# Moving the turning and summing of rows behind the ninth output product in a fused attention and mixture-of-experts kernel

## The chip, the cores and the metric

One core of one Trainium2 chip runs the whole kernel. The metric is device time in microseconds (us); lower is better. Names of engines are those of the profile: PE is TensorE (PEld its weight loads), DVE is VectorE, ACT is ScalarE, POOL is GpSimd, SP is the engine that issues the large loads. PE's granted clock of 1.00 is 2.4 GHz, 0.50 is 1.2 GHz.

## What is computed

The reference is attention followed by a mixture of experts with one expert per token, all in float32:

```
x = attention(q, k, v)                  # 8 batches, 8 heads, 576 positions, 64 features; heads 0-3 see a window
                                        # of 32 positions, heads 4-7 every fourth of 128 positions
logits = x @ w_gate                     # x: 8 x 576 tokens of 512 features; 8 experts
e = argmax(logits)  or the expert of the token before it, where sigmoid(x @ w_local) >= 0.5
out = softmax(logits)[e] * (relu(x @ w1[e]) @ w2[e])     # w1[e] 512 x 1024, w2[e] 1024 x 512
```

## The kernel before, in words

The first part (about 160 us) is attention and routing. Each token's row of x is written to a table `xd` in memory. The rest is the experts' work, on which this document dwells.

**Units.** Tokens are sorted by expert and cut into 19 units, each of one expert. The planner at L872 to L888 lists them in a fixed order: units 0 to 3 are pairs (256 tokens), 4 full (128), 5 half (64), 6 quad (512), 7 quart (32), 8 quad, 9 full, 10 quad, 11 half, 12 quart, 13 quad, 14 full, 15 quad, 16 quart, 17 quad, 18 quart. Below, H8 is the hidden layer of unit 8 and O8 its output layer. Weights lie in two slots, even units in one and odd units in the other; SP loads the next unit of a slot (2 MB for w1, 2 MB for w2) as soon as the present one has been used (L900).

**Order.** The loop at L1536 goes over units u from 2 on and emits: H of u (`run_hidden`), then `features(u + 1)`, then `gather_more`, then O of u - 1 (`run_output`). So a quad's output comes after the hidden layer of the small unit that follows it, and ahead of the next quad's hidden layer. PE and DVE run what they are given in the order in which it is emitted (L222 exempts these two from the scheduler); the order on POOL, ACT and SP is chosen by a scheduler.

**Products.** Quads multiply with seven products of half size in place of eight (`chain`, L1059). An output of a quad is two such chains over three accumulators x, y, z (L1285), 14 products in all. The fifth product of a chain adds to x; `finish(3)` (DVE, L1309) reads x; the seventh product adds to x again and so must wait for that read. Operands that are sums are made on DVE: sums of w1 (`sum`, L958 to L961, 128x1024), of w2 (`sum`, L964 to L967), of hidden rows (`hc`, L958 to L961, 128x512), of input rows (`xcq`, L964 to L967, 128x512). Of the second chain's `hc`, two sums are made behind the third product and two behind the sixth (L1278).

**Rows.** `features(u)` (L1055) first calls `turn_rows` (L1026): it issues whatever gathers of unit u are still waiting (`fetch_all`), then DVE turns the rows (`xe<-xg`, L1037, four instructions of 128x512 for a quad, one per 128 tokens), and then `sums_of_rows` makes four `xcq` sums. The second product of a quad's hidden layer needs the first `xcq` sum, which needs all four turned blocks.

**Gathers.** The rows of a quad come from `xd` by 16 gathers (`fetch`, L988), each a tiny DVE memset (L999) and an indirect DMA issued by POOL (L1000). Gathers wait in one list in order of units. Behind every product there is a gap (`work_gap`, L939), which may put one sum on DVE and then gives the list a credit, 2 for large units and 1 for small ones, kept to at most 5; a gather costs 3 (L1014). `gather_more(done)` (L1005) lets further units into the list while those beyond `done` need no more than 9 buffers (a quad needs 4, other late units 1):

```
while following[0] < NU and sum(map(need, range(done + 1, following[0] + 1))) <= XG:
    gather(following[0])
    following[0] += 1
```

**Sums of w1** for the next quad are given to `run_output` as `push`, behind 14 empty steps, so that they fall behind products 10, 11 and 14 (two of them there).

Of the kernel before, what the change touches and what calls it, by code (L numbers as in the profile page):

```python
# [72 lines left out]
EARLY, FIRST = 2, 2  # L73
# [145 lines left out]
def whole(ctx, tc, exact, bad, qk, v, wgl, w1, w2, con, msk, qmk, out, cst, wg, ones):  # L219
# [664 lines left out]
    units = [dict(kind="pair", col=2 * i, late=False) for i in range(FIRST)]  # L884
# [3 lines left out]
    NU = len(units)  # L888
# [11 lines left out]
    def weights(u, second):  # L900

        i = units[u]["slot"]
        loads.add((u, second))
        if not second:
            units[u]["held"] = holds.get(i)
            holds[i] = nc.values_load(of_unit(u, "experts", rows=1), engines=[ET.SP], min_val=0, max_val=E - 1,
                                      skip_runtime_bounds_check_because="clamped to the experts")
            units[u]["expert"] = holds[i]
        e, held = units[u]["expert"], units[u]["held"]
        w, s, pattern = (w2, raw2, "p m f -> p (m f)") if second else (w1[u >= TURNED], raw1, "p m k f -> p (m k f)")  # L910
        if not second and u >= TURNED and units[u]["before"] < TURNED:
            held = None
        if second and not units[u]["late"] and isinstance(held, int):
            held = None
        more = {} if held is None else dict(cond=e != held, cond_hint=False)
        nc.sync.dma_start(out=s[i].rearrange(pattern), in_=w[bass.ds(e, 1)].rearrange("o p x -> (o p) x"), **more)
# [6 lines left out]
    def next_weights(*did):  # L923

        ready.update(did)
        if "late" in ready:
            for w in [w for w in follow if w in ready]:
                follow.remove(w)
                weights(after[w[0]], w[1])

    def gap(time=3):
        fetch_some(time)
        for steps in waiting, behind:
            if steps:
                f = steps.pop(0)
                if f:
                    f()

    def work_gap(sums=True, time=2):  # L939
        for _ in range(len(soon) > 4 and 2 or len(soon) > 0 if sums else 0):  # L940
            soon.pop(0)()
        gap(time)

    def now(push):
        for f in push:
            f()

    def flush():
        while soon:
            soon.pop(0)()  # L950
# [30 lines left out]
    def gather(u):  # L981


        for j, n in enumerate({"quad": (NQS,) * 4, "pair": (NQS, NQS), "full": (NQS,), "half": (ROW // SQ,), "quart": (1,)}[units[u]["kind"]]):
            for q in range(2 if u < TURNED else n):
                fetches.append((u, lambda u=u, j=j, q=q: fetch(u, j, q)))
# [18 lines left out]
    def gather_more(done):  # L1005

        def need(u):
            return {"quad": 4, "pair": 2}.get(units[u]["kind"], 1)
# [4 lines that stand above are left out]
# [13 lines left out]
    def turn_rows(u):  # L1026
        kind = units[u]["kind"]
        rows = {"half": ROW, "quart": SQ}.get(kind, P)
        assert u >= TURNED or kind == "pair"
        fetch_all(u)  # L1030
        xe[u] = [mw.tile([P, DK, 2 * P], F32, name="xe") for _ in range(2 if kind == "quad" else 1)]
        for j in range({"quad": 4, "pair": 2}.get(kind, 1)):
            x = xg.pop((u, j))
            to = xe[u][j // 2][:, :, j % 2 * P:j % 2 * P + rows]
            if u >= TURNED:
                x = x.rearrange("p g (q f) -> p (g q) f", f=P)
                nc.vector.transpose(to.rearrange("p k (q t) -> p k q t", t=SQ),  # L1037
                                    x[:, :rows // SQ].rearrange("p q (k d) -> p k q d", k=DK))
                continue
            x = x.rearrange("p g f -> p (g f)")  # L1040
            tp = bank([P, DK, P], "tp")
            for kk in range(DK):
                nc.tensor.transpose(tp[:, kk], x[:, kk * P:(kk + 1) * P], ident)
            nc.scalar.copy(to, tp)

    def sums_of_rows(u):
        if not units[u]["seven"]:
            return []
        if units[u]["kind"] == "quad":
            xc[u] = stage.tile([P, 4, DK // 2, 2 * P], F32, name="xcq", bufs=1)  # L1050
            return sums_right(xc[u], *(xe[u][j][:, 2 * k:2 * k + 2] for k in range(2) for j in range(2)))
        xc[u] = mw.tile([P, 4, DK // 2, P], F32, name="xc", bufs=1)
        return sums_right(xc[u], *(xe[u][0][:, 2 * k:2 * k + 2, j * P:(j + 1) * P] for k in range(2) for j in range(2)))

    def features(u):  # L1055
        turn_rows(u)
        now(sums_of_rows(u))
# [146 lines left out]
    def turned(u):  # L1204

        h = ht[u]
        n = 2 if units[u]["kind"] == "half" else 1
        ts = h[:, 0:n].rearrange("p m t -> p (m t)")
        tp = bank([P, 2 * n, P], "ht")
        for c in range(2 * n):  # L1210
            nc.tensor.transpose(tp[:, c], ts[:, c * P:(c + 1) * P], ident)
        nc.scalar.copy(h[:, 2:2 + n].rearrange("p m (c t) -> p (m c) t", t=P), tp)
# [219 lines left out]
    def register(value, most, why):  # L1432
        return nc.values_load(value, min_val=0, max_val=most, skip_runtime_bounds_check_because=why)
# [23 lines left out]
    def run_hidden(u, push):  # L1457
        soon.extend(push)
        for k, fits in enumerate(hidden(u)):
            work_gap(fits, 2 if is_large(u) else 1)  # L1460
            if u == FIRST and k == 1:
                early_sums[u] = sums_of_weights(u, True)
                soon.extend(early_sums[u][:2])
            if u == FIRST and k == 4:
                turn_rows(u + 1)
        flush()
        if u < FIRST:
            next_weights((u, False))
        elif after[u] is not None:
            weights(after[u], False)  # L1470

    def run_output(u, push):
        soon.extend(push)
        for k, fits in enumerate(output(u)):
            work_gap(fits, 2 if is_large(u) else 1)
            if u == NU - 2 and k == 4:
                turned(u + 1)
        if u == NU - 2 and k < 4:
            turned(u + 1)
        flush()  # L1480
        if u < FIRST:
            next_weights((u, True))
        elif after[u] is not None:
            weights(after[u], True)

    def is_large(u):
        return FIRST <= u < NU and units[u]["kind"] in ("pair", "quad") or 0 <= u < FIRST

    def before_it(u):
        return max((t for t in range(u) if is_large(t)), default=-2)  # L1490

    def both(u):
        if not is_large(u):
            return []
        sums = units[u]["sums"]
        if u > TURNED - 1 and before_it(u) < u - 1:
            return list(sums)
        if u in early_sums:
            return sums[:2] + [early_sums[u][2]] + sums[2:] + [early_sums[u][3]]
        return [f for two_ in zip(sums, sums_of_weights(u, True)) for f in two_]  # L1500
# [32 lines left out]
    def wait(gaps):  # L1533
        return [lambda: None] * (2 * gaps)

    for u in range(FIRST, NU):  # L1536
        own = is_large(u) and u >= TURNED and before_it(u) < u - 1
        run_hidden(u, (both(u - 1) if u > FIRST else []) + (wait(5) + sums_of_weights(u, True) if own else []))
        if u > FIRST and u + 1 < NU:
            features(u + 1)  # L1540
        gather_more(min(u + 1, NU - 1) if u > FIRST else FIRST)
        push = [f for t in when.get(u, []) for f in
                wait((7 if units[u - 1]["kind"] == "quad" else 5) if is_large(u - 1) else 0) + sums_of_weights(t, False)]
        if u > FIRST:
            run_output(u - 1, push)
        else:
            now([f for two_ in zip(sums_of_rows(u + 1), sums_of_weights(u + 1, False)) for f in two_])
        if units[u]["kind"] in ("half", "quart") and u < NU - 1:
            turned(u)
        if u in (FIRST + 3, FIRST + 4) and not exact:  # L1550
            next(checks)
        if u == FIRST + 6 and not exact:
            again = register(bad[0:1, 0:1], 1, "a comparison's result")
    now(both(NU - 1))
    run_output(NU - 1, [])
    return again

# [58 lines left out]
```

## Time and profile before

| | |
|---|---|
| median of 3 runs | 645.85 us (644.46 to 646.57) |
| profiled execution | 645.84 us, of which the span of the trace is 643.9 us |
| PE busy in the span | 604.5 us (94%) |
| DVE, POOL, ACT busy | 360.5, 226.0, 176.2 us |
| mean granted clock of PE | 0.983 |

How to read it: PE is busy nearly throughout, so other engines matter where PE waits for them. "Busy" for PE also covers matmuls at half clock. In the rows below, the first number is the start in us from the start of the span, the second the duration; x8 means that eight like instructions are merged, and the bracket tells how long the engine sat idle before and what ended that.

### The profile page before, as it was taken

The numbers are of one execution on the slowest core, as the hardware profiler recorded it, in microseconds if no ns is written. First come the engines' busy times: TensorE is split into PE (matmuls) and PEld (weight loads), VectorE is DVE, ScalarE is ACT, GpSimd is POOL, SyncE is SP. The second block draws the span as 40 slices with busy tenths as digits, with TensorE's granted clock in tenths as the row PEclk, the third lists the DMA queues.
The fourth block names the chain that finished last, engine by engine and source line by source line (L and its number), as shares of the span: only waits on it lengthen the run. The fifth ranks groups of instructions, "written<-read, shape, count | busy, mean of one in ns | idle before, by whom it ended". The sixth has DMA issues, their size and how long they took to land.

```text
span 643.9 us, 13952 instructions
## 1 busy us (share of the span) xinstructions
PE 604.5 (94%) x5678; PEld 511.2 (79%) x5678; DVE 360.5 (56%) x902; ACT 176.2 (27%) x320; POOL 226.0 (35%) x219
## 2 busy tenths in 40 slices
PE   6879988879999998999979999999999999999995
PEld 6767777668888998868768898868789888688884
DVE  3757889989697384374344464434445535443521
ACT  2555544342211331113112311221132113112310
POOL 3232142223014644463256335444543451011011
PEclk8989989999999999999979999999999999999998
DMA  9989988398001247251835192454554650734131
GB/s 348 406 319 294 346 278 299 122 344 342 15 34 35 82 161 262 84 202 26 351 122 188 49 387 76 174 175 164 167 206 160 285 188 31 274 159 163 43 127 42
DMA packets 28442, 121.18 MB, mean 188 GB/s; under 512 B 4748, under 2 KB 15116, under 8 KB 22992
## 3 DMA queue, kind: packets, MB, share of 16 engines
q1 hardware_dynamic: 20800, 101.04, 42.9%
q0 software_dynamic: 7568, 19.15, 8.8%
q8 instruction: 47, 0.77, 0.5%
q14 instruction: 27, 0.22, 0.1%
HBM read 120.17 MB, written 19.14 MB: 216 GB/s over the span
## 4 chain that ended last, share of the span: by engine, by line
PE 79%; DVE 10%; issue 4%; DMA 3%; ACT 1%; POOL 1%; SPq 1%; another core or an unknown queue 0%; DVEq 0%; POOLq 0%
PE yp L1293 29%; PE hp L1179 23%; PE hp L1121 3%; PE pv L410 3%; PE yp L1269 3%; PE hp L1147 3%; PE sc L348 3%; PE hp L1136 2%; PE tp L429 2%; DVE pr L354 2%; DVE x L415 1%; PE yp L1253 1%; PE yp L1234 1%; PE hp L1098 1%; DMA vt<-in_v_dram 1%
## 5 line engine op out<-in xcount | busy, mean ns | idle before, releaser
L1000 POOL DMA_INDIRECT xg<-xd,at x116 | 117.8, 1015 | 144.4 <-DVE xg L999 115.8
L1293 PE MATMUL yp<-sum,hc 128*128 128x256 f32 x384 | 88.7, 380 | 1.6 <-ACT y L1302 1.6
L1293 PEld LDWEIGHTS yp<-sum,hc 128*128 128x128 f32 x384 | 72.7, 190 | 11.8 <-ACT y L1302 2.0
L1222 POOL DMA_INDIRECT out_dram<-y,tok x35 | 43.5, 1242 | 97.3 <-DVE y L1309 43.3
L1309 DVE SCALAR_TENSOR_TENSOR y<-yp,gate,y 128x256 f32<-128x256 f32 x48 | 23.1, 484 | 89.9 <-PE yp L1293 62.1
L1179 PE MATMUL hp<-xcq,sum 128*128 128x256 f32 x288 | 64.1, 379 | 0.0
L1293 PE MATMUL yp<-raw,h 128*128 128x256 f32 x256 | 62.0, 386 | 0.0
L1179 PEld LDWEIGHTS hp<-xcq,sum 128*128 128x128 f32 x288 | 54.7, 190 | 7.4
L357 ACT ACTIVATE pr<-pr 128x512 f32<-128x512 f32 x64 | 43.8, 684 | 60.0 <-DVE pr L354 56.9
L1293 PEld LDWEIGHTS yp<-raw,h 128*128 128x128 f32 x256 | 48.7, 193 | 8.6 <-issue 2.0
L354 DVE SCALAR_TENSOR_TENSOR pr<-sc,mk 128x512 f32<-128x512 f32 x64 | 45.4, 748 | 16.9 <-PE sc L348 15.4
L410 PE MATMUL pv<-vt,pr 128*64 128x65 f32 x1152 | 44.9, 231 | 9.8 <-issue 5.8
L410 PEld LDWEIGHTS pv<-vt,pr 128*64 128x64 f32 x1152 | 39.3, 143 | 13.2 <-issue 7.7
L1195 DVE TENSOR_TENSOR h<-hp,h 128x512 f32<-128x512 f32 x36 | 24.3, 689 | 41.8 <-PE hp L1179 41.8
L1179 PE MATMUL hp<-xe,raw 128*128 128x256 f32 x192 | 43.4, 379 | 0.0
L1179 PEld LDWEIGHTS hp<-xe,raw 128*128 128x128 f32 x192 | 36.2, 190 | 4.8
L1302 ACT ACTIVATE y<-yp,gate 128x256 f32<-128x256 f32 x48 | 22.7, 474 | 61.7 <-PE yp L1293 54.4
L348 PE MATMUL sc<-kq 64*64 64x96 f32 (+3 forms) x1280 | 34.3, 246 | 5.2 <-DVE pr L354 2.8
L289 POOL COPY vt<-vt 64x1040 f32<-64x1040 f32 x16 | 17.3, 1080 | 57.6 <-DMA vt<-in_v_dram 38.8
L348 PEld LDWEIGHTS sc<-kq 64*64 64x64 f32 x1280 | 28.8, 136 | 10.7 <-DVE pr L354 4.0
L1000 POOL DMA_INDIRECT xg<-xd,row x16 | 18.2, 1140 | 52.9 <-DVE xg L999 20.6
L1306 ACT ACTIVATE y<-yp,gate 128x256 f32<-128x256 f32 x16 | 7.6, 475 | 105.7 <-PE yp L1293 105.7
(261 smaller groups left out, 976.6 us busy)
## 6 DMA issues: line engine op xcount, KB each, us to landing
raw<-in_w_dram SPq DMA_DIRECT2D x38, 2048.0 KB
kq<-in_qk_dram SPq DMA_DIRECT2D x13, 1184.0 KB
vt<-in_v_dram SPq DMA_DIRECT2D x15, 650.0 KB
xd<-x SPq DMA_DIRECT2D x16, 512.0 KB
kq<-in_qk_dram SPq DMA_DIRECT2D x6, 592.0 KB
xg<-xd,at POOLq DMA_INDIRECT x116
xd<-x SPq DMA_DIRECT2D x32, 32.0 KB
vt<-in_v_dram SPq DMA_DIRECT2D x2, 325.0 KB
```

The lines of the kernel that those rows point to most:

```text
L348: nc.tensor.matmul(sc[c:c + QB, u, lo - a * QB:hi - a * QB], lhsT=kt[h, WIN + j * QB:WIN + (j + 1) * QB], rhs=qt[h, lo:hi], start=True, st ...
L354: nc.vector.scalar_tensor_tensor(to, sc[:, :, :w], -CEIL, mk[:, at:at + w].unsqueeze(1).to_broadcast([P, 2, w]), Alu.max, Alu.min)
L357: nc.scalar.activation(to, to, Act.Exp, scale=SCALE)
L410: nc.tensor.matmul(pv[half * QB:(half + 1) * QB, k - a], lhsT=pr[:, u, (i - a) * QB:(i - a + 1) * QB], rhs=vt[:, slot(i), u], start=True, ...
L1000: nc.gpsimd.indirect_dma_start(out=to, out_offset=None, in_=of, in_offset=bass.IndirectOffsetOnAxis(ap=place, axis=0))
L1121: nc.tensor.matmul(to, lhsT=w[:, m, kk], rhs=x[:, kk, :P], start=(kk == 0), stop=(kk == DK - 1))
L1179: nc.tensor.matmul(to[v][:, m], lhsT=a[:, 2 * v + m, kk], rhs=b[:, kk], start=first and m == 0 and kk == 0, stop=(kk == DK // 2 - 1), skip ...
L1195: nc.vector.tensor_tensor(to, of[v], to, op=Alu.add)
L1222: nc.gpsimd.indirect_dma_start(out=rows_of_out(), out_offset=bass.IndirectOffsetOnAxis(ap=of_unit(u, "tok", j), axis=0), in_=y, in_offset= ...
L1293: nc.tensor.matmul(to, lhsT=a[:, m], rhs=b[:, m], start=first and m == 0, stop=(m == FK // 2 - 1), skip_group_check=True)
L1302: nc.scalar.activation(at(k), of, Act.Copy, scale=of_unit(u, "gate", 2 * s + k // 2))
L1309: nc.vector.scalar_tensor_tensor(at(k), of, of_unit(u, "gate", 2 * s + k // 2), at(k), Alu.mult, Alu.add)
```

## The change

`features(u + 1)` is no longer emitted ahead of O of u - 1 where both u - 1 and u + 1 are quads. It is emitted within that output, behind its ninth product (and behind that product's gap). This holds for u = 7, 9, 14 and 16, that is for the rows of units 8, 10, 15 and 17 in O6, O8, O13 and O15. The rows of units 6 and 13 stay where they were. In the four places `gather_more` is called with u in place of u + 1.

```diff
-    def run_output(u, push):
+    def run_output(u, push, rows_of=None):
         soon.extend(push)
         for k, fits in enumerate(output(u)):
             work_gap(fits, 2 if is_large(u) else 1)
+            if rows_of and k == 8:
+                features(rows_of)
...
-        if u > FIRST and u + 1 < NU:
+        within = u + 1 < NU and units[u + 1]["kind"] == units[u - 1]["kind"] == "quad"
+        if u > FIRST and u + 1 < NU and not within:
             features(u + 1)
-        gather_more(min(u + 1, NU - 1) if u > FIRST else FIRST)
+        gather_more(u if within else min(u + 1, NU - 1) if u > FIRST else FIRST)
...
-            run_output(u - 1, push)
+            run_output(u - 1, push, u + 1 if within else None)
```

## Rows read from the trace of the kernel before

**Rows 1.** The page: busy time of PE

```profile
PE 604.5 (94%) x5678; PEld 511.2 (79%) x5678; DVE 360.5 (56%) x902; ACT 176.2 (27%) x320; POOL 226.0 (35%) x219
```

**Rows 2.** Timeline of PE from the start of O6 to the start of H8

```profile
312.59 1.99 PE L1293 MATMUL yp<-raw,h 128*128 128x256 f32 x8
...
326.50 3.78 PE L1293 MATMUL yp<-sum,h 128*128 128x256 f32 x8 [3.28 <-DVE xg L999]
...
343.20 0.38 PE L1211 MATMUL ht<-cst,h 128*128 128x128 f32 x2
```

**Rows 3.** Timeline of DVE in the same stretch

```profile
320.87 0.71 DVE L1037 STREAM_TRANSPOSE xe<-xg 128x512 f32<-128x512 f32 x1 [4.90 <-issue]
...
324.17 0.69 DVE L958 TENSOR_TENSOR hc<-h 128x512 f32<-128x512 f32 x1
...
325.97 0.88 DVE L1309 SCALAR_TENSOR_TENSOR y<-yp,gate,y 128x256 f32<-128x256 f32 x2
```

**Rows 4.** Timeline of POOL: the last gather of unit 8

```profile
313.43 0.99 POOL L1000 DMA_INDIRECT xg<-xd,at  x1 [0.30 <-issue]
```

**Rows 5.** Stretches: PE, PEld, DVE, ACT, POOL busy (count), granted clock, DMA share, GB/s

```profile
35.00:36.00 1.00, 1.00 (x15) 0.88 (x15) 0.21 (x2) 0.00 (x0) 0.00 (x0) 0.61 1.13 406
38.00:39.00 1.00, 1.00 (x40) 1.00 (x36) 0.19 (x1) 0.41 (x2) 0.94 (x2) 0.69 0.97 402
242.00:243.00 1.00, 0.16 (x1) 0.00 (x0) 0.00 (x0) 0.00 (x0) 0.00 (x0) 1.00 0.66 193
243.00:244.00 1.00, 0.21 (x1) 0.21 (x2) 0.00 (x0) 0.74 (x2) 0.00 (x0) 1.00 0.85 360
325.00:326.00 1.00, 0.00 (x0) 0.00 (x0) 1.00 (x4) 0.00 (x0) 0.69 (x2) 0.67 0.04 16
332.00:333.00 1.00, 1.00 (x5) 0.85 (x5) 0.00 (x0) 0.00 (x0) 0.78 (x1) 0.91 0.22 66
```

**Rows 6.** The chain that ended last: O13, whole

```profile
500.61 24.18 PE yp L1293 x112
```

**Rows 7.** Timeline of DVE in O15: turning and summing of a quad without a wait

```profile
559.06 2.48 DVE L1037 STREAM_TRANSPOSE xe<-xg 128x512 f32<-128x512 f32 x4
...
564.12 0.68 DVE L958 TENSOR_TENSOR hc<-h 128x512 f32<-128x512 f32 x1
```

**Rows 8.** Timeline of DVE in O13

```profile
512.70 1.22 DVE L958 TENSOR_TENSOR sum<-raw 128x1024 f32<-128x1024 f32 x1
512.71 1.21 DVE L999 MEMSET xg<- 1x1 f32 x3
519.70 0.48 DVE L1309 SCALAR_TENSOR_TENSOR y<-yp,gate,y 128x256 f32<-128x256 f32 x1 [5.78 <-issue]
```

**Rows 9.** Timeline of POOL in O13

```profile
513.36 1.40 POOL L1000 DMA_INDIRECT xg<-xd,at  x1 [0.30 <-issue]
515.07 1.02 POOL L1222 DMA_INDIRECT out_dram<-y,tok  x1 [0.31 <-ACT y L1302]
...
517.67 0.95 POOL L1000 DMA_INDIRECT xg<-xd,at  x1 [0.30 <-issue]
```

**Rows 10.** Timeline of POOL around the end of O10

```profile
457.75 0.95 POOL L1000 DMA_INDIRECT xg<-xd,at  x1 [2.92 <-DVE xg L999]
...
464.73 0.98 POOL L1000 DMA_INDIRECT xg<-xd,at  x1 [0.30 <-issue]
```

**Rows 11.** Stretches there (columns as in Rows 5)

```profile
459.00:460.00 1.00, 1.00 (x6) 0.87 (x6) 0.69 (x2) 0.00 (x0) 0.94 (x1) 1.00 0.22 66
...
472.00:473.00 1.00, 1.00 (x6) 0.89 (x5) 0.00 (x0) 0.57 (x1) 0.70 (x1) 1.00 1.06 451
```

**Rows 12.** Timeline of PE: the second product of H13

```profile
470.50 7.07 PE L1179 MATMUL hp<-xcq,sum 128*128 128x256 f32 x32
```

**Rows 13.** DMA queues from 467.0 to 468.0 us: packets, MB, share of 16 engines

```profile
q0 software_dynamic: 93, 0.29, 74.3%
```

## The prediction

> **What bounds the kernel now.** I read the page's busy times first: PE works 604.5 of 643.9 us [rows 1], so a change elsewhere counts only where PE waits. Then the chain of waits from unit 6 on, where quads alternate with small units. Of the four outputs that the change touches, three (O8, O13, O15) run as one unbroken block, 24.18 us for 14 products in O13 [rows 6], which is 1.727 us a product. O6 alone is broken, and the timelines of PE and DVE say how. O6 starts at 312.59; its seventh product is due six products later, at 322.95, and starts at 326.50 [rows 2], 3.55 us late. It waits for the DVE read of x behind the fifth product, and DVE comes to that read only at about 326 [rows 3], because the turning of unit 8 stands ahead of it. The fourth block turned waited 4.90 us, to 320.87 [rows 3], and the gather it needs was issued by POOL at 313.43 [rows 4], so about 7.0 us passed from issue to landing, if some 0.4 us of the 7.44 is the wake-up.
>
> A broken block costs more than its gap. The granted clock falls during the gap to 0.50 (1.2 GHz) and is back at 1.00 only in the stretch from 332 on [rows 5]. O6 should have ended 24.18 us after its start, at 336.77; the instructions behind it start at 343.20 [rows 2]. The loss is 6.43 us: 3.55 of gap and 2.88 of slow clock.
>
> **The change part by part.** No instruction is added or dropped, and PE's order stays. Eight DVE instructions per place move, and gathers move with them.
>
> *O6.* With `features(8)` out of the way, DVE meets the reads of the first chain in time. The sixth product ends at 322.95; a read (0.4, half of 0.88) and two `hc` sums (0.6 each, a little under their 0.69 because they overlap) [rows 3] follow, so turning begins at about 324.6, when all gathers have landed (320.5). Turning and four sums of a quad take from 559.06 to 564.12, 5.06 us [rows 7], then one w1 sum 1.2 [rows 8]: DVE is free at 330.9. The eleventh product ends at 312.59 + 11 x 1.727 = 331.6, so its read is not late; the read that the fourteenth product needs comes at 333.4, and that product is due at 335.04. Gain: **-6.43 us**. The margins there are 0.7 and 1.2 us.
>
> *O8 and O15.* The same arithmetic holds, with gathers landed long before: no cost. The 5.06 us go into an idle time of DVE behind the ninth product like the 5.78 us before the read at 519.70 [rows 8]. If that cover were gone, the fourteenth product would wait.
>
> *The list of gathers.* This is the hidden part. With `gather_more(9)` in place of `gather_more(10)`, units 10, 11 and 12 need 6 of 9 buffers, and 13 no longer fits. Its 16 gathers enter the list not ahead of O8 but behind H10. I count credits from there, starting at the full 5: O9 gives 8 gaps of 1, so 4 gathers (the cap swallows one credit); H11 one, with 1 credit left; O10 has 28 + 1 credits, 9 gathers; H12 one. That is 15: the sixteenth is issued by `features(13)` itself. Before, all were out in H10. Unit 14's four and unit 15's sixteen queue behind. O11 issues 1, H13 10, H14 3, and the nine gaps of O13 that precede `features(15)` issue the last 6, the very last in the gap just ahead of it. So two places get a fresh wait for a gather.
>
> *O13.* DVE runs ahead: the memsets for the gaps behind products 6, 7 and 9 go out at about 512.7, as three did before [rows 8]. POOL then took a gather at 513.36, a send at 515.07 and two gathers, the last at 517.67 [rows 9]; the emitted pattern is the same, so unit 15's last gather starts at 517.67. The loads are quiet there. A gather issued in quiet at 457.75 [rows 10] had its traffic in the stretch 459 to 460 [rows 11], so at most 2.25 us. Landing: about 520.0. Then the fourth block and four sums, 320.87 to 324.17 = 3.30 us [rows 3], a w1 sum 1.2, a read 0.4, a second w1 sum 1.2, and the read of x 0.4: 526.5. The fourteenth product was due at 500.61 + 13 x 1.727 = 523.06. Gap: 3.45 us, nearly that of O6. The slow clock behind it: the low stretch after O6's gap cost 2.88; another lasted only from about 35.2 to 38.4 [rows 5], which would cost 1.6. I take 2.88, from the row whose gap is alike, and keep 1.6. Cost: **+6.33 us** (5.05 to 6.33).
>
> A rule bears on the gather at 513.36, which took 1.40 us where its like takes 0.95, while DVE ran a w1 sum [rows 8, 9]. The Trainium skill, SBUF — State Buffer, "SBUF: two separate sides", has a VectorE operation with two SBUF inputs lock a port that GpSimd shares; turning has one input. By that rule POOL would be 0.45 us earlier here and the forecast 646.5; by the rows alone nothing changes, and I leave it out.
>
> *H13.* At the end of O10 POOL took six operations, a gather of 0.98 us at 464.73 the last [rows 10]; after the change that one is unit 13's fifteenth, and with 0.3 us between two operations the sixteenth follows at 466.0. Two bounds for its landing: 2.2 us in quiet, at 468.2; 7.0 us as under load in O6, at 473.0, for the loads keep the DMA share near 1 to 473 [rows 11]. Yet between two loads, 467 to 468, the gathers' queue has 74% of the engines [rows 13] and drains. I take 470.3, nearer that row. The fourth block (0.7) and a sum of its size (0.7) make it about 471.7; so the second product of H13, due at 470.50 [rows 12], is about 1.3 us late with 0.1 for a semaphore. A PE gap of 1.6 us at 242 to 244 left the clock at 1.00 [rows 5], so no more is charged. Cost: **+1.3 us** (0 to 3.9 and a slow clock of 2.88, so 6.8).
>
> *Sum.* -6.43 + 6.33 + 1.3 = +1.2. Against the profiled execution's 645.84 us, 0.01 under the median: **647.0 us**. What is won in O6 is paid back in O13.
>
> **The rivals.** *Faster: O13 does not pay.* POOL's order is a scheduler's. Put the three gathers ahead of the send and the last starts at about 516; PE resumes about 1.7 us sooner, the gap is 1.75 us and about at the length that left the clock alone: -6.43 + 1.75, with 0 to 1.3 at H13, 641.2 to 642.5. With no new wait at all it is 639.4. For it: the four instructions lie ready within a microsecond. Against: the scheduler put the send between in the trace [rows 9].
>
> *Slower: the last gather of unit 13 lands as late as the one in O6.* It costs once it lands later than about 469. At 7.0 us from issue PE waits 3.9 and loses 2.88 by its clock: 647.0 - 1.3 + 6.8 = 652.5. For it: loads fill the engines on both sides. Against: the drain at 467. The Trainium skill, DMA: Bandwidth & Descriptors, "Queues, rings and completion order", says that each DMA engine takes turns between queues, packet by packet. By that rule a gather of eight rows per engine would wait behind eight packets of a load, as the 7.0 us bear out; the 74% at 467 shows what happens without a load, and this one straddles both.
>
> *The change does not do what it says.* O6's fourteenth product inherits the wait, because its margin of 1.2 us is overdrawn by late DVE work; then there is little gain and the costs stay: about 653.
>
> **How the numbers follow.** A measurement of this kernel tells about 0.3% (1.9 us) from no change. Likeliest, 0.44: both O13 and H13 as summed, 645.0 to 647.8 with the smaller clock loss and H13 between 0.7 and 2.1; this is the case of no change. O13 does not pay: 0.24, faster. Late landing at H13: 0.22, slower. No gain in O6 or another wait unseen: 0.10, slower. The range takes the first three in, 641.0 to 652.5.
>
> **What would show it.** Right: O6 one block of 24.2 us; in O13 the last product starts about 3.4 us late, behind a DVE read that follows `xcq` sums, with the granted clock at 0.50 behind it; a gather of unit 13 as the last one ahead of its turning, and a short PE gap after the first product of H13. Wrong: no gap in O13 (then faster), a gap of 3 us or more in H13 (then slower), or a gap left in O6.

## The result, and the profile after

| | before | after |
|---|---|---|
| median of 4 runs | 646.21 us (644.46 to 652.06) | 652.65 us (651.66 to 657.87) |
| ratio, with its 95% interval | | 1.0104 (1.0070 to 1.0138) |
| profiled execution; its span | 645.84; 643.9 us | 651.66; 649.8 us |

The change makes the kernel slower by about 1%. The forecast was 647.0, with a range of 641.0 to 652.5. The page of the kernel after, busy times:

```profile
PE 606.3 (93%) x5678; PEld 513.6 (79%) x5678; DVE 360.1 (55%) x902; ACT 176.4 (27%) x320; POOL 226.5 (35%) x219
```

Against [rows 1] PE is busy 1.8 us longer with the same instructions, so some run at a lower clock, and in a span 5.9 us longer it idles 4.1 us more. The chain that ended last tells where:

```profile
312.08 24.37 PE yp L1293 x112
336.67 24.18 PE hp L1179 x112
...
459.19 8.35 DMA xg<-xd,at
...
517.42 2.46 DMA xg<-xd,at
...
526.50 3.62 PE yp L1293 x8
...
563.09 24.40 PE yp L1293 x112
```

O6 is now one block, and H8 starts at 336.67. Two new links are gathers: one of 8.35 us ahead of H13, one of 2.46 us in O13. The timeline of PE at both places (as in Rows 2, the bracket is the idle time before an instruction and what ended it):

```profile
460.22 3.62 PE L1179 MATMUL hp<-xe,raw 128*128 128x256 f32 x16
469.15 8.61 PE L1179 MATMUL hp<-xcq,sum 128*128 128x256 f32 x32 [5.31 <-DVE xcq L964]
...
491.50 1.95 PE L1253 MATMUL yp<-raw,h 128*32 128x128 f32 x64
...
500.63 1.89 PE L1293 MATMUL yp<-raw,h 128*128 128x256 f32 x8
...
526.50 3.62 PE L1293 MATMUL yp<-sum,h 128*128 128x256 f32 x8 [3.26 <-DVE xg L999]
529.92 3.71 PE L1179 MATMUL hp<-xe,raw 128*128 128x256 f32 x16
```

H13's second product is the late one. From the start of H13 to that of O12 it takes 31.28 us where the unbroken block takes 24.27, so 7.0 us are lost. From the start of O13 to that of H15 it takes 29.29 us against 24.18 [rows 6], so 5.1 us. O6 gives back 6.3: from its start to what follows took 30.61 us [rows 2] and takes 24.28. The sum, -6.3 + 7.0 + 5.1 = +5.8, accounts for the 5.9 us by which the span grew. The timeline of DVE, which PE waits for, and of POOL, which DVE waits for:

```profile
324.40 2.51 DVE L1037 STREAM_TRANSPOSE xe<-xg 128x512 f32<-128x512 f32 x4
...
331.38 0.48 DVE L1309 SCALAR_TENSOR_TENSOR y<-yp,gate,y 128x256 f32<-128x256 f32 x1 [0.67 <-PE yp L1293]
...
459.19 0.95 POOL L1000 DMA_INDIRECT xg<-xd,at  x1 [0.30 <-issue]
...
467.66 0.71 DVE L1037 STREAM_TRANSPOSE xe<-xg 128x512 f32<-128x512 f32 x1 [8.87 <-DMA xg<-xd,at]
...
513.54 0.98 POOL L1000 DMA_INDIRECT xg<-xd,at  x1 [0.30 <-issue]
...
517.42 0.96 POOL L1000 DMA_INDIRECT xg<-xd,at  x1 [0.30 <-issue]
...
520.00 0.71 DVE L1037 STREAM_TRANSPOSE xe<-xg 128x512 f32<-128x512 f32 x1 [5.16 <-DMA xg<-xd,at]
```

In O6 the four blocks are turned without a wait, in place of the 4.90 us of [rows 3], and DVE comes to the read at 331.38 before PE does. At H13 the last gather of unit 13 is issued at 459.19 and its rows are turned at 467.66; the 0.1 us of the wake-up taken off, about 8.4 us. At O13 the last gather of unit 15 is issued at 517.42 and turned at 520.00, 2.6 us later.

Why 8.4 us in one place? The DMA queues show it (q0 carries gathers and sends, q1 the loads of weights; packets, MB, share of 16 engines; one answer for each of the stretches 456 to 457, 460 to 461, 461 to 462, 463 to 464 and 458 to 468):

```profile
q1 hardware_dynamic: 24, 0.39, 96.8%
...
q0 software_dynamic: 99, 0.29, 76.8%
q1 hardware_dynamic: 14, 0.13, 31.6%
...
q1 hardware_dynamic: 23, 0.31, 73.5%
q0 software_dynamic: 32, 0.09, 22.4%
...
q1 hardware_dynamic: 21, 0.34, 80.2%
q0 software_dynamic: 23, 0.04, 10.7%
...
q1 hardware_dynamic: 192, 2.65, 66.2%
q0 software_dynamic: 256, 0.72, 18.5%
```

Two sends and three gathers are issued from 453.25 to 459.19, and their 256 packets pass from 458 to 468 (the last two gathers of unit 15 are 64 packets, so 32 a gather, which leaves 80 a send). Nothing of q0 passes at 456 to 457, beside the first load. In the gap before the next load 99 pass in one microsecond, as in [rows 13]. Then the next load runs, and q0 gets 32 and 23 packets a microsecond. The last gather's 32 are behind all the others.

PE's clock behind the two gaps (columns as in Rows 5):

```profile
469.00:470.00 1.00, 0.85 (x2) 0.76 (x3) 0.97 (x3) 0.00 (x0) 0.00 (x0) 0.50 0.00 0
...
526.00:527.00 1.00, 0.50 (x2) 0.41 (x3) 1.00 (x6) 0.00 (x0) 0.26 (x1) 0.85 1.03 426
```

At 469 PE runs at 0.50 (1.2 GHz). H13's second product is 5.48 us late (due at 463.67), so of the 7.0 us about 1.5 are slow clock; O13's fourteenth is 3.42 late (due at 500.63 + 13 x 1.727 = 523.08; 1.727 us is one product), so of its 5.1 about 1.7.

### The profile page after: what moved, and what is told of

Same layout as the page of the kernel before. It is cut to its first block, busy times and chain, and to the rows that moved or that the text cites. A ratio compares the mean times of both kernels' runs of the same rounds, so it can differ in the third digit from the quotient of the medians.

```text
span 649.8 us, 13955 instructions
## 1 busy us (share of the span) xinstructions
PE 606.3 (93%) x5678; PEld 513.6 (79%) x5678; DVE 360.1 (55%) x902; ACT 176.4 (27%) x320; POOL 226.5 (35%) x219
## 4 chain that ended last, share of the span: by engine, by line
PE 70%; DVE 12%; issue 9%; POOL 4%; DMA 4%; another core or an unknown queue 0%; ACT 0%; SPq 0%; DVEq 0%; POOLq 0%
PE yp L1293 25%; PE hp L1179 19%; PE pv L410 4%; PE yp L1269 3%; PE hp L1147 3%; PE sc L348 3%; POOL xg L1000 3%; PE tp L429 2%; PE hp L1121 2%; DVE pr L354 2%; PE hp L1136 2%; DMA xg<-xd,at 2%; DVE x L415 1%; DMA vt<-in_v_dram 1%; PE hp L1098 1%
## 5 line engine op out<-in xcount | busy, mean ns | idle before, releaser
L1179 PE MATMUL hp<-xcq,sum 128*128 128x256 f32 x288 | 65.7, 385 | 5.3 <-DVE xcq L964 5.3
L410 PE MATMUL pv<-vt,pr 128*64 128x65 f32 x1152 | 46.6, 236 | 9.4 <-issue 5.4
L410 PEld LDWEIGHTS pv<-vt,pr 128*64 128x64 f32 x1152 | 41.0, 148 | 12.9 <-issue 7.4
```

The source lines that it names most:

```text
L410: nc.tensor.matmul(pv[half * QB:(half + 1) * QB, k - a], lhsT=pr[:, u, (i - a) * QB:(i - a + 1) * QB], rhs=vt[:, slot(i), u], start=True, ...
L1179: nc.tensor.matmul(to[v][:, m], lhsT=a[:, 2 * v + m, kk], rhs=b[:, kk], start=first and m == 0 and kk == 0, stop=(kk == DK // 2 - 1), skip ...
```

## Experiments

The chips of these runs timed the kernel before at 641.9 to 642.6 us, so that only ratios to it are compared across the tables. The theory was: O6's gain is real; both losses are late gathers, made late because `gather_more(u)` admits unit 13's gathers after H10; and at H13 the price is set by the load that the gather runs beside.

**The move in O6 alone, and the four moves with a longer list.** In the first kernel only unit 8's rows move; in the second all four do, and the list may hold gathers for 11 buffers in place of 9. (`exact` in the diffs is false in the body of the program that ran here.)

```diff
-        within = u + 1 < NU and units[u + 1]["kind"] == units[u - 1]["kind"] == "quad"
+        within = (exact or u == 7) and u + 1 < NU and units[u + 1]["kind"] == units[u - 1]["kind"] == "quad"
```

> Only the rows of unit 8 are moved behind the ninth product of O6; units 10, 15 and 17 and the list of gathers stand as in the kernel before. Theory (the move pays in O6, and the loss comes from late gathers of units 13 and 15): O6 is one block of 24.2 us, H13 and O13 have no PE gap, and the time is 6.4 us below the kernel before, about 639.5. Rival (the moved DVE work crowds the reads of the second chain wherever it is put, O6 too): a PE gap ahead of the fourteenth product of O6, and a gain under 3 us.

```diff
-XG = 9
+XG = 11
```

> The whole change, with 11 gather buffers in place of 9, so that units 13 and 14 enter the list of gathers ahead of O8 again. The last gather of unit 13 is then issued within H10 and that of unit 15 within H13. Theory (late gathers): no PE gap in H13 or O13, the four moves cost nothing of themselves, and the time is that of moving unit 8 alone, 639 to 640. Rival (the DVE work itself is too much behind the ninth product): H13 heals, but the fourteenth product of O13, and perhaps of O8 and O15, still starts 3 us late; 645 or more.

Measured: 0.9883 (0.9851 to 0.9916) and 0.9907 (0.9872 to 0.9942), 635.06 and 635.14 us where before took 641.89. The chain of the second shows H13 and O13 as blocks without a gap (O6 at 307.60 and O15 at 545.52 are blocks of 24.37 too):

```profile
455.03 24.18 PE hp L1179 x112
...
488.44 24.18 PE yp L1293 x112
```

O8, at 365.59, is a block of 24.18. So turning behind the ninth product costs nothing of itself in any of the four places. What costs is the list. (The time expected for the first kernel in microseconds is off by as much as that chip ran faster; the ratio is as expected.)

**The list alone, rows unmoved.** The kernel before, with the new argument of `gather_more` only.

```diff
-        gather_more(min(u + 1, NU - 1) if u > FIRST else FIRST)
+        within = u + 1 < NU and units[u + 1]["kind"] == units[u - 1]["kind"] == "quad"
+        gather_more(u if within else min(u + 1, NU - 1) if u > FIRST else FIRST)
```

> The kernel before, in which only the call that lets units into the list of gathers is made as in the changed kernel; no DVE work is moved. Theory (the list alone makes the loss): the gap in H13 is there as in the changed kernel, 5 us and 7 us with the slow clock; O6 keeps its loss of 6.4 us; and unit 15's rows, turned ahead of O13, wait for six gathers issued at that point, which holds up the first chain of O13 by another 4 to 7 us: 656 to 660. Rival (the loss comes from the moved DVE work): the time stays within 2 us of the kernel before.

Measured: 1.0291 (1.0261 to 1.0322), 659.98 us: 18 us lost, more than expected. Its timeline of PE has three gaps, O6's old one, H13's and O13's:

```profile
323.01 3.78 PE L1293 MATMUL yp<-sum,h 128*128 128x256 f32 x8 [4.09 <-DVE xg L999]
...
472.13 10.19 PE L1179 MATMUL hp<-xcq,sum 128*128 128x256 f32 x32 [6.04 <-DVE xcq L964]
...
522.31 3.78 PE L1293 MATMUL yp<-sum,h 128*128 128x256 f32 x8 [6.59 <-DVE y L1309]
```

H13's loss thus needs no moved row. Both losses were undersized in the expectation. From the start of H13 to that of O12 it takes 33.6 us, 9.3 more than the block, where 7 were expected. Unmoved, the turning of unit 15 waits for the same gathers ahead of O13's own sums, and O13 takes 32.9 us, 8.7 more than its block.

**The second load held back.** After, with the loads of weights of units 12, 13 and 14 asked for only in O11, behind three one-element copies on DVE; the gathers stay as late as they were.

```diff
         elif after[u] is not None:
-            weights(after[u], False)
...
+        elif u == 10 and not exact:
+            return
+        elif u == 11 and not exact:
+            for t in raw2[0][0:1, 0, 0:1], raw1[0][0:1, 0, 0, 0:1], raw2[1][0:1, 0, 0:1]:
+                nc.vector.tensor_copy(t, t)
+            weights(12, True)
+            weights(14, False)
+            weights(13, True)
```

(and `run_hidden` leaves unit 14's load to it.)

> The whole change; the loads of w2 for units 12 and 13 and of w1 for unit 14 are made to wait (by a copy of one element onto itself on DVE) until DVE has turned and summed the rows of unit 13. The last gather of unit 13 is issued at the same point as in the changed kernel. Theory (that gather is late because the two loads hold the DMA engines): it lands 2 to 3 us after its issue in place of 8.4, the gap of 5.3 us in H13 shrinks to under 0.5, O13 keeps its gap of about 3.3 us, and the time is about 7 us below the changed kernel's 652.4, so 645 to 646. Rival (it is late because it is issued last, whatever the loads do): the gap in H13 stays near 5 us and the time at 652.

Measured: 0.9981 (0.9951 to 1.0012), 640.68 us. The timeline of POOL, PE and DVE at H13, and of PE in O13:

```profile
453.63 0.95 POOL L1000 DMA_INDIRECT xg<-xd,at  x1 [0.30 <-issue]
...
456.22 0.71 DVE L1037 STREAM_TRANSPOSE xe<-xg 128x512 f32<-128x512 f32 x1 [4.60 <-DMA xg<-xd,at]
...
458.11 7.07 PE L1179 MATMUL hp<-xcq,sum 128*128 128x256 f32 x32
...
514.01 2.51 PE L1293 MATMUL yp<-sum,h 128*128 128x256 f32 x8 [3.35 <-DVE xg L999]
```

The gather is as late as in after (1.0 us ahead of H13's first product in both, 454.65 and 460.22), yet it lands within 2.6 us in place of 8.4, and the gap at H13 is gone. So the loads beside it set the price, and not that it is the last to be issued. From the start of H6 to the end, which leaves out the first part, it takes 359.4 us against after's 367.4. O13's gap, beside no load, stays.

**One, two and five places earlier.** After, with more credit in gaps of O10: three, six, or all of them give 3 in place of 2.

```diff
-            work_gap(fits, 2 if is_large(u) else 1)
+            work_gap(fits, 3 if u == 10 and k < 3 and not exact else 2 if is_large(u) else 1)
```

(`k < 6` in the second, no bound on k in the third.)

> The whole change; the first three gaps of O10 give one credit more, so that the last gather of unit 13 is issued one place earlier (about 457.9 on the changed kernel's clock, not 459.2). Theory A (what is queued before the first load ends goes through between the two loads, at 460 to 461): it lands by about 463 and the gap in H13 falls from 5.3 us to about 1. Theory B (under these loads a gather takes about 8 us from issue): it lands at 466.3 and the gap falls by 1.3 us only, to about 4. O13 as in the changed kernel, a gap of 3.3 us, for its last gather is still in the ninth gap.

> As the run before, with six gaps of O10 in place of three: two places earlier in H13, and in O13 the last gather is issued one gap earlier. Theory A: gap in H13 under 1 us. Theory B: about 2.7 us. In O13 the last gather starts at most one POOL operation (1.3 us) earlier, so the gap there falls from 3.3 to about 2.0 us.

> As the two runs before, with all 14 gaps of O10 at a credit of 3: the last gather of unit 13 is issued in the gap behind the eleventh product of O10, that of unit 15 behind the third product of O13. Both theories: no gap in H13 (A) or under 1 us (B), none in O13; the time is that of moving unit 8's rows alone, 1.0 to 1.2% below the kernel before. A gap that stays in O13 would mean that the moved DVE work itself is too much there.

Measured: 1.0097 (1.0068 to 1.0125), 0.9967 (0.9940 to 0.9994) and 0.9885 (0.9843 to 0.9927). The first missed both theories' gaps in H13 (about 1 and about 4 us). Its timeline of PE, DVE and POOL:

```profile
453.88 0.98 POOL L1000 DMA_INDIRECT xg<-xd,at  x1 [0.30 <-issue]
...
464.01 0.71 DVE L1037 STREAM_TRANSPOSE xe<-xg 128x512 f32<-128x512 f32 x1 [10.85 <-DMA xg<-xd,at]
465.51 8.59 PE L1179 MATMUL hp<-xcq,sum 128*128 128x256 f32 x32 [5.69 <-DVE xcq L964]
```

The gather was issued 2.3 us ahead of H13's first product (456.20) in place of 1.0, and PE's gap did not shrink (5.69 us, after 5.31): this gather took 10 us. The DMA queues, 457 to 458 and 459 to 460:

```profile
q1 hardware_dynamic: 22, 0.34, 80.3%
q0 software_dynamic: 22, 0.07, 17.2%
...
q1 hardware_dynamic: 21, 0.34, 80.5%
q0 software_dynamic: 19, 0.07, 18.0%
```

In these two stretches q0 gets about as many packets as the load does, one for one. The gather still stands behind both sends: 224 packets of q0 pass from 454 to 463.7, only 46 of them in the microsecond between the two loads, where after had 99. With two places the gather comes ahead of the last send (449.12 against 450.40) and PE's gap is 1.82 us, between the two theories' "under 1" and 2.7; O13's fell to 2.11, about as expected:

```profile
459.47 7.17 PE L1179 MATMUL hp<-xcq,sum 128*128 128x256 f32 x32 [1.82 <-DVE xcq L964]
```

With all of O10's credits raised, H13 and O13 are both one block, and the whole gain of O6 is kept, as both theories had it.

**The two sends behind the gather.** After, with the sends of O10's second chain issued only behind unit 13's rows (each behind a one-element copy on DVE).

```diff
+        if u == 10 and j < 2 and not exact and not now_:
+            late_sends.append((y, u, j))
+            return
...
+        if u == 12:
+            for y, of, j in late_sends:
+                nc.vector.tensor_copy(y[0:1, 0:1], y[0:1, 0:1])
+                send(y, of, j, True)
```

> The whole change; the two sends of results that O10's second chain gives to POOL are made to wait (by a copy of one element onto itself on DVE) until DVE has turned and summed the rows of unit 13, so that unit 13's last three gathers have no send ahead of them in their queue. The loads stand as in the changed kernel. Theory C (the queue's packets take turns with the load's, one for one, so what counts is how many are ahead: 256 in the changed kernel, of which two sends of 80 and three gathers of 32, at some 23 per us beside a load and 99 in the gap between two loads): 96 are left, which the gap between the loads takes; the last gather lands about 3 us or more earlier against H13, and the gap of 5.3 us in H13 falls under 1 us; O13 keeps its 3.3 us; the ratio to the kernel before falls from 1.010 to about 0.998. Theory D (the gather lands when the second load ends, whatever is queued): the gap stays at 5 us and the ratio at 1.010.

Measured: 1.0002 (0.9973 to 1.0031), 641.46 us against 642.22. The timeline of POOL, DVE and PE:

```profile
451.44 0.94 POOL L1000 DMA_INDIRECT xg<-xd,at  x1 [0.30 <-DVE xe L1037]
...
458.13 0.71 DVE L1037 STREAM_TRANSPOSE xe<-xg 128x512 f32<-128x512 f32 x1 [6.30 <-DMA xg<-xd,at]
459.62 7.17 PE L1179 MATMUL hp<-xcq,sum 128*128 128x256 f32 x32 [1.14 <-DVE xcq L964]
```

The gap is 1.14 us, where the theory of packets ahead said under 1 and its rival 5. The gather took 6.6 us and landed while the second load still ran (it ended at about 459.9), so a gather need not wait for a load to end: it waits for the packets ahead of it, at the rate that the load leaves. Deferring the sends also brought the gather forward, 3.4 us ahead of H13. Four kernels together part the two (the first load's first packet passes at 453.1 in after, 449.2 one place earlier, 447.2 two places earlier and 448.0 here):

| | after | one place | two places | sends behind |
|---|---|---|---|---|
| last gather of unit 13 issued, us behind the first load's first packet | 6.1 | 4.7 | 1.9 | 3.4 |
| its landing, us behind the same packet | 14.4 | 14.7 | 10.6 | 10.0 |
| packets of q0 issued since, its own included | 256 | 224 | 112 | 96 |

One place earlier, the gather was issued 1.4 us sooner into the load and landed no sooner. With the sends behind it was issued 1.5 us later than with two places and landed 0.6 us sooner. So the moment of issue does not set the landing, and what stands in the queue ahead does. The count gives it only roughly: 224 packets took no less than 256 (46 of them passed in the gap between the loads, 99 in after), and with two places 155 packets had passed when the gather landed, where 112 would do in strict order. O13's gap stays (3.41 us).

**The kernel before, with unit 8's gathers paced faster.** No row is moved; H6's gaps give 3 in place of 2.

```diff
-            work_gap(fits, 2 if is_large(u) else 1)
+            work_gap(fits, 3 if u == 6 and not exact else 2 if is_large(u) else 1)
```

> The kernel before, without the move: only the gaps of H6 give the list of gathers a credit of 3 in place of 2, so that the last gather of unit 8 is issued three gaps before the end of H6 and not in H7. Theory (O6 waited for a late gather; the move only hides it): the turning of unit 8 ahead of O6 no longer waits, O6 is one block of 24.2 us and the time is that of moving unit 8's rows, 1.0 to 1.2% below the kernel before. Rival (O6 was slow because eight DVE instructions stand ahead of its first reads, however early the rows are there): a gap of 1 us or more stays in O6 and the gain is under 0.5%.

Measured: 0.9878 (0.9835 to 0.9920), 635.82 us. O6 is one block and its turning waits for nothing, ahead of the first product as in before (one line of the chain and one of DVE's timeline):

```profile
309.15 24.37 PE yp L1293 x112
```

```profile
310.56 2.48 DVE L1037 STREAM_TRANSPOSE xe<-xg 128x512 f32<-128x512 f32 x4
```

So O6's loss before was itself a late gather. The move hides it; issuing the gather earlier removes it, for the same gain and with no change of when a unit enters the list. The four kernels without a gap (the move in O6 alone, the longer list, all of O10 paced faster, this one) lie from 0.9878 to 0.9907, and their intervals overlap: none is shown to be the best.

## Why the prediction was wrong

**O6, -6.43: right.** It gained 6.33. Turning began at 324.40 (forecast 324.6 on a clock on which O6 starts 0.6 later), and the read behind it had 0.67 us to spare where 0.7 was forecast. The cause given was right too: DVE's read stood behind a turning that waited for a gather.

**O8 and O15, nothing: right.** In after O8 is one block of 24.18 us and O15 one of 24.40, and the longer list shows that turning there is covered.

**The list: right in its count.** The count gave fifteen gathers by H12, the sixteenth issued by `features(13)`, and unit 15's last one in the gap ahead of its turning. Each is where the count put it, and the list alone makes both losses.

**O13, +6.33: right in its mechanism, mis-sized in its clock.** The last gather came at 517.42 (forecast 517.67), the rows were turned at 520.00 (forecast 520.0; the exact hit is luck, as the gather came 0.25 us earlier and landed after 2.46 us where 2.25 were forecast), the last product is 3.42 us late (forecast 3.45). The loss is 5.1, because the slow clock cost 1.7 and not 2.88; the row of the early stretch, 1.6, was the nearer one. "Faster: O13 does not pay" fell: the scheduler kept the send between the gathers.

A word on the port. The gather that took 1.40 us at 513.36 beside a w1 sum [rows 9] takes 0.98 at 513.54, where DVE is turning. The Trainium skill, SBUF — State Buffer, "SBUF: two separate sides", lets a VectorE operation with two inputs in SBUF lock the port pair that it shares with GpSimd, against a GpSimd operation that reads SBUF (a gather reads its row numbers there). The pair agrees, and it is not the only one. In the trace of before, from 190 us on, 23 gathers were issued while a sum of two SBUF operands had at least 0.15 us to run, and every one ends 0.81 to 0.85 us after that sum (at 285.36, 390.51 and 411.28 they take 1.33, 1.47 and 1.79 us). Gathers issued while DVE turns take 0.95 to 0.98 us, and beside sums that take one operand from PE's results 0.94 to 0.95. So the 0.45 us that the prediction left out was there: counted from the start of O13 (500.44 and 500.63), the last gather came 0.44 us earlier than in before.

**H13, +1.3: wrong, and it decides the case.** It cost 7.0. The step that failed is "between two loads, 467 to 468, the gathers' queue has 74% of the engines [rows 13] and drains. I take 470.3, nearer that row." The point of issue was right: 459.19 is 466.01 on the prediction's clock, on which H13 starts 6.82 later, and 466.0 was forecast. The landing was wrong: 467.54 is 474.4 on that clock. The row was right too: after has the same burst, 99 packets in one microsecond. But 256 packets were to pass, and at the end of the gap, at 461, 127 were left with the last gather's 32 at their end. These had to go beside the next load, at some 32 a microsecond, then 23, and fewer at the end, until 467. The question was how many packets stand ahead, and not what share the queue has in a quiet microsecond. The upper bound of 473.0 was too low as well: its 7.0 us came from one gather under load, and this one took 8.4. (The 0.4 us of wake-up that it takes off the 7.44 stand in no run; from this landing to the turning 0.12 pass.) And in the +1.3 the slow clock was put at nothing, from a gap of 1.6 us that left it at 1.00 [rows 5]; the gap is 5.3, and the clock costs 1.5. The run with the loads held back shows the load as the cause, and the four kernels beside each other show that what stands ahead in the queue counts.

"Slower: the last gather of unit 13 lands as late as the one in O6" is what came about. Its 652.5 stands against 651.66 in the profiled execution: H13 lost 7.0 and not 6.8, O13 5.1 and not 6.33. The 6.8 are near by luck: 3.9 of wait and 2.88 of slow clock were priced, 5.5 and 1.5 came. The median, 652.65, lies just beyond the range.

The Trainium skill, DMA: Bandwidth & Descriptors, "Queues, rings and completion order", has each DMA engine take turns between queues, packet by packet. The 22 to 22 and 21 to 19 packets a microsecond beside the second load agree. The eight packets of a load that the prediction drew from it are not borne out: a gather is 32 packets, two an engine, and the 7.0 us in O6 were not its turns alone. From 316 to 321 of before, 80 packets of q0 passed, 48 of them from the send issued ahead of it at 311.60. What the rule does not account for stands below.

## What to carry to other kernels

Moving a consumer later in one engine's order can also move what a shared list admits: count, place by place, which transfer is now issued last ahead of its use, on every queue. Price a late gather by the packets that stand ahead of it in its queue and by the load that runs beside them; one empty microsecond does not stand for the whole wait. Where a consumer waits for a late transfer, issue the transfer earlier before moving the consumer: here a credit of 3 in place of 2 in one stage gave the whole gain of about 1.2%. It has to come early enough to pass what it would queue behind: one place earlier gave nothing at H13.

## What the runs showed of the hardware

The time of a gather of 32 packets from issue to use depends on its neighbours by a factor of four: 2.6 us with the loads held back, 6.6 to 10 us beside loads of 2 MB.

At the beginning of a load that follows a quiet stretch, the gathers' queue got no packets at all for some microseconds, and only later about one for one. With the sends behind, gathers were issued at 447.89 (in 1.70 us) and 450.19; the queues at 451 to 452 and 456 to 457 (packets, MB, share):

```profile
q1 hardware_dynamic: 26, 0.43, 102.3%
...
q1 hardware_dynamic: 24, 0.39, 96.0%
q0 software_dynamic: 21, 0.06, 15.3%
```

With the loads held back, q0's first packet came 0.6 us after POOL was done with its issue (449.44 and 450.0). For an issue just ahead of a load or in its first 2 us it took 3.2 to 3.9 us, in six kernels (in after 455.01 and 458.6, in before 459.95 and 463.8). In five of them some 105 of the load's 144 packets had gone by then, in before 76, so the queue does not start at one fixed place in the load. Turns packet by packet alone do not explain the wait. Why the packets start so late was not tried and stays open; it is a part of the 10 us that the single place earlier could not shorten.

Idle times of PE of like length were followed by different losses of clock: 3.3 us in O6 before by 2.9 us, 3.3 us in O13 after by 1.7, 5.3 us at H13 by 1.5.
